# Attention with memory slots feeding a SiLU feed-forward: two weight tiles loaded into the unwritten half of w_in's tile, conversions moved into the prologue, Exp's table load ahead of k and v

## The chip, the cores and the metric

One core of one Trainium2 chip runs the whole kernel. The metric is the device time of one execution in microseconds (us), the median of a few runs. The kernel before takes 720.51 us (three runs, 720.13 to 721.42).

## The reference

```python
# q, k, v: [8, 8, 576, 64], phi: [8, 8, 576, 32], all float32
a = exp(phi - max(phi, axis=2)); a = a / (sum(a, axis=2) + 1e-9)   # softmax over the sequence
k_m = einsum('bhsm,bhsd->bhmd', a, k)                              # 32 memory slots per head
v_m = einsum('bhsm,bhsd->bhmd', a, v)
scores = matmul(q, k_m.T) / sqrt(64)
attn = softmax(scores, axis=-1)                                    # over the 32 slots
x = matmul(attn, v_m) -> [8 * 576, 512]                            # heads side by side
h = x @ w_in                                                       # [512, 2048]
out = (h * sigmoid(h)) @ w_out                                     # [2048, 512]
```

## The kernel before, in words

The kernel goes batch by batch (8 batches of 576 tokens), and within a batch over 16 slots `fc` of 128 feed-forward columns each. Instead of forming x, it multiplies w_in by v's memory first: `p_mm` (L540) makes the projection of a piece of w_in on PE into the PSUM tile `bg`, and `p_split` (L560) takes it to SBUF as a high part (ACT, L564) and a low part (DVE, L566), `pparts`. `ffn1` (L570) multiplies these with the high and low parts of the attention weights (`aparts`) into the PSUM tile `h`, of which there is one; `act` (L593) applies SiLU on ACT (`g`, `gleft`) and `split` (L586) makes `gparts` on DVE; `ffn2` (L605) multiplies these with `wo_hi` and `wo_lo` into `acc`. Each slot issues `ffn1` of its own columns, then `ffn2` of the slot before in two halves, and after each half the extra work that the table `events` holds for that slot (half slots are written .5).

The weights come as 64-bit words that hold float64 numbers. A weight tile ("i", j) or ("o", j) is 256 of w_in's columns or of w_out's rows, 1 MB in memory; there are eight of each kind. `w_load` (L120) loads a tile, or one half of it (`part`), into a buffer `raw`; there are three such buffers (`RAWB`), which the tiles use in turn. `w_conv` (L142) makes float32 of it in steps: step 0 is two ACT passes (L158, L159), step 1 two DVE passes (L162, L163). For w_out, a copy of the high part follows on ACT (L165) and, in step 2, a subtraction on DVE for the low part (L167). w_in's result goes into `win`, a constant tile for all 16 column groups, w_out's into `wo_hi` and `wo_lo`. `load_next` and `conv_next` (L172, L177) go through the tiles from j = 1 on in the order i1, o1, i2, o2, and so on; each `conv_next` loads a further tile behind its conversion. Loads with `few` set wait for the fifth load before them (`DEEP`).

Batch 0's attention, the prologue (L694 to L754), has a written order. `phi` is loaded through SP, k and v through ACT's queue, then q and the first weights through SP as `LOADS` (L43) lists them: i0 in two halves, both halves of q, o0 in two halves, and L, which is tile i1. Softmax over phi (`phi_max`, `phi_allmax`, `phi_sub`, `phi_exp`), the contraction with k and v (`e_mm`), the scores (`f_scores`, `f_copy`, `f_turn`), their softmax (`f_max`, `f_sub`, `f_exp`, `f_sum`, `f_norm`) and the way back (`f_back`, `f_high`, `f_low`) follow; `keep_warm` issues matmuls whose result isn't used. The instructions of PE and of SP keep the order of the text everywhere, those of DVE and ACT in the prologue; behind it, a planner orders DVE and ACT. Batch 1's attention is spread over the slots of batch 0, and so on for each batch. In batch 0 the tile of k and v is used in turn by `f_copy` too (tag `kv`).

Of the events of batch 0, these bear on the weights: the projection of w_in's tile j in slot max(1, 2j - 1.5); the second half of o0 in slot 0; the k-th `conv_next` (k from 0 to 13) in slot k.

Of the kernel before, what the change touches and what calls it, by code (L numbers as in the profile page):

```python
# [10 lines left out]
F32 = mybir.dt.float32  # L11
# [3 lines left out]
I64 = mybir.dt.int64  # L15
AF = mybir.ActivationFunctionType
# [3 lines left out]
P = 128  # L20
B, S, H, M, D = 8, 576, 8, 32, 64
HM = H * M
NR = H // 2
KVW = 2 * D + 1
DMODEL, DFF = 512, 2048
# [14 lines left out]
PHW = FULLC * HM + P  # L40
KVC = 2 * NR * KVW
RAWB = 3
LOADS = "i0 Q0 Q1 i1 o0 o1 L"  # L43
DEEP = 5


# [1 line left out]
def attn_ffn_kernel(  # L48
# [9 lines left out]
    nc = tc.nc  # L58
    const = ctx.enter_context(tc.tile_pool(name="const", bufs=1))
    sb = ctx.enter_context(tc.tile_pool(name="sb", bufs=2))  # L60
# [3 lines left out]
    ident = const.tile([P, P], F32, name="ident")  # L64
# [11 lines left out]
    def keep_warm(t, n):  # L76
        for _ in range(n):
            nc.tensor.matmul(
                t, dummy[:, :P], dummy.unsqueeze(1).broadcast_to([P, 2, 2 * P]),
                start=True, stop=True, skip_group_check=True,  # L80
            )
# [38 lines left out]
    def w_load(w, part=None, few=False):  # L120


        kind, j = w
        if w not in raws:
            shape = [P, 2, NR * P] if kind == "i" else [P, 2, DMODEL]
            raws[w] = sb.tile(shape, I64, tag="raw", name="raw", bufs=RAWB)
        if kind == "i":
            for k in range(2) if part is None else (part,):
                f = (2 * j + k) * P
                load(  # L130
                    raws[w][:, k].rearrange("p (r f) -> p r f", r=NR),
                    w_in[:, f : f + P].rearrange("(r p) f -> p r f", p=P),
                    few,
                )
        else:
            src = w_out[j * CW : (j + 1) * CW, :].rearrange("(r p) f -> p r f", p=P)
            load(w_part(raws[w], part), w_part(src, part), few)
# [4 lines left out]
    def w_conv(w, part=None, steps=(0, 1, 2)):  # L142
        kind, j = w
        words = raws[w].bitcast(U32).rearrange("p r (f t) -> p r f t", t=2)
        low, high = (w_part(words[:, :, :, t], part) for t in range(2))
        r = low.bitcast(I32)
        fc = slice(2 * j, 2 * j + 2) if part is None else slice(2 * j + part, 2 * j + part + 1)
        if kind == "i":
            to = win[:, fc].rearrange("p k r f -> p k (r f)")
            a = to.bitcast(I32)  # L150
        else:
            to = high.bitcast(F32)
            if 0 in steps:
                n, tag = (2, "cva") if part != 1 else (1, "cva1")
                cvas[w, part] = sb.tile([P, n, DMODEL], I32, tag=tag, name="cva", bufs=1)[:, : 2 if part is None else 1]
            a = cvas[w, part]
        if 0 in steps:
            nc.scalar.activation(a.bitcast(F32), high.bitcast(F32), AF.Prelu, scale=2.0**-112, alpha=-(2.0**32))  # L158
            nc.scalar.activation(r, low, AF.Copy, scale=2.0**-29)  # L159
        if 1 in steps:  # L160
            au = a.bitcast(U32)
            nc.vector.tensor_scalar(au, au, 3, None, op0=ALU.logical_shift_left)  # L162
            nc.vector.tensor_tensor(to.bitcast(I32), a, r, op=ALU.add)  # L163
            if kind == "o":
                nc.scalar.activation(wo_hi[:, fc], a.bitcast(F32), AF.Copy)  # L165
        if 2 in steps and kind == "o":
            nc.vector.tensor_tensor(wo_lo[:, fc], to, wo_hi[:, fc], op=ALU.subtract)  # L167

    to_load = iter([(k, j) for j in range(1, DFF // CW) for k in "io"])
# [2 lines left out]
    def load_next(few=False):  # L172
        w = next(to_load, None)
        if w is not None:
            w_load(w, None, few)
# [27 lines left out]
    def load_kv(b):  # L203
        queue = nc.scalar if b == 0 else None
        ts = []
        for c in range(FULLC):
            t = sb.tile([P, 2, NR, KVW], F32, tag="kv", name=f"kv{b}_{c}", bufs=FULLC)
            load(t.rearrange("p g r f -> p (g r f)"), kv[b, :, c * KVC : (c + 1) * KVC], queue=queue)
            ts.append(t)
        t = sb.tile([P, NR, KVW], F32, tag="kr", name=f"kr{b}", bufs=1)  # L210
        load(t.rearrange("p r f -> p (r f)"), kv[b, :, FULLC * KVC :], queue=queue)
        at[b]["kv"], at[b]["kr"] = ts, t

    def load_q(b, hf, few=False):
        t = sb.tile([P, NR, HALF], F32, tag="q", name=f"q{b}_{hf}", bufs=2)
        at[b]["q", hf] = t
        load(t.rearrange("p r s -> p (r s)"), qT[b, hf], few)
# [225 lines left out]
    def f_copy(u):  # L443
        if u == 0:
            first["left"] = sb.tile([P, P], F32, tag="mx", name="sleft", bufs=1)
        t = first["main", u] = sb.tile([P, 2, 2 * P], F32, tag="kv", name=f"sT{u}", bufs=FULLC)
        left = first["left"]
        nc.scalar.copy(t, first["st", u][:, :, : 2 * P])
        nc.scalar.copy(left.rearrange("p (g h f) -> p g h f", g=2, h=2)[:, :, u], first["st", u][:, :, 2 * P : HALF])

    def f_turn(u):
        main = first["main", u]
        if u == 0:
            t = ps.tile([P, 512], F32, tag="acc", name="firstu", bufs=NI)
        else:
            t = ps.tile([P, 2, 512], F32, tag="h", name="firstu", bufs=1).rearrange("p b f -> p (b f)")
        for c in range(2):
            for g in range(2):
                n = 2 * c + g
                nc.tensor.transpose(t[:, n * P : (n + 1) * P], main[:, g, c * P : (c + 1) * P], ident)  # L460
        if u:
            nc.tensor.transpose(t[:, 2 * HM : 2 * HM + P], first["left"], ident)
        first["ps", u] = t
# [23 lines left out]
    def f_sub(u):  # L487
        nc.vector.tensor_tensor(
            f_groups(f_sc(u)), f_groups(first["ps", u][:, : UW[u]]), f_bc(f_part(u, "mx", 2 * S // M), u),
            op=ALU.subtract,  # L490
        )

    def f_exp(u):
        nc.scalar.activation(f_sc(u), f_sc(u), AF.Exp, scale=SCALE)
# [36 lines left out]
    def f_low(u):  # L531
        nc.vector.tensor_tensor(f_to("alo", u), first["aT", u], f_to("ahi", u), op=ALU.subtract)
# [27 lines left out]
    def p_split(b, f, w, bg, steps=(0, 1)):  # L560
        hi, lo = pj[b, f // JW]
        c = slice(f % JW, f % JW + w)
        if 0 in steps:
            nc.scalar.activation(hi[:, :, c], bg[:, :, :w], AF.Copy)  # L564
        if 1 in steps:
            nc.vector.tensor_tensor(lo[:, :, c], bg[:, :, :w], hi[:, :, c], op=ALU.subtract)  # L566
# [71 lines left out]
    def ev(b, slot, fn, *a):  # L638
        events.setdefault((b, slot), []).append((fn, a))

    for b in range(B):
# [38 lines left out]
        if n + 1 < B:  # L680
            ev(b, sk, load_phi, n + 1)
        ev(b, 14, p_mm, n, 0, JW)
    ev(0, 0, w_conv, ("o", 0), 1)
    for k in range(DFF // CW * 2 - 2):
        ev(0, k, conv_next)

# [3 lines left out]
    whole = ExitStack()  # L692
    whole.enter_context(in_order(PE, SP))
    load_phi(0)  # L694
    load_kv(0)
    for c in LOADS.split():
        if c[0] == "Q":
            load_q(0, int(c[1]), True)
        elif c[0] == "L":
            load_next(True)  # L700
        else:
            w_load((c[0], 0), int(c[1]), True)
    w = [(("i", 0), 0), (("i", 0), 1), (("o", 0), 0)]
    idle = ps.tile([P, 2, 512], F32, tag="h", name="idle", bufs=1)[:, 0]
    with in_order(DVE, ACT) as last:
        keep_warm(idle, 9)
        for p in range(2):
            phi_max(0, (p,))
            phi_allmax(0, (p,))
            keep_warm(idle, (7, 8)[p])  # L710
        for p in range(2):
            phi_sub(0, (p,))
            phi_exp(0, (p,))
        e_mm(0)
        w_conv(*w[0], (0,))
        keep_warm(idle, 4)
        f_tr()
        w_conv(*w[0], (1,))
        keep_warm(idle, 2)
        f_scores(0)  # L720
        f_copy(0)
        f_turn(0)
        f_scores(1)
        f_copy(1)
        f_vt()
        f_turn(1)
        f_max(0)
        f_sub(0)
        f_exp(0)
        bg = p_mm(0, 0, P, False)  # L730
        spare = first["spare"] = ps.tile([P, 512], F32, tag="acc", name="spare", bufs=NI)
        keep_warm(spare, 10)
        f_max(1)
        f_sub(1)
        f_exp(1)
        nc.scalar.activation(tiny[:, :1], ident[:, :1], AF.Silu)
        f_sum(0)
        p_split(0, 0, P, bg, (0,))
        w_conv(*w[1], (0,))
        f_norm(0)  # L740
        f_back(0)
        f_sum(1)
        w_conv(*w[2], (0,))
        f_high(0)
        f_norm(1)
        f_back(1)
        p_split(0, 0, P, bg, (1,))
        f_low(0)
        f_high(1)
        f_high(2)  # L750
        f_low(1)
        f_low(2)
        w_conv(*w[1], (1,))
        w_conv(*w[2], (1, 2))  # L754
    load_phi(1)
    load_kv(1)
    load_q(1, 0)
# [87 lines left out]
```

## Time and profile before

| | |
|---|---|
| median of three runs | 720.51 us |
| the profiled execution | 721.51 us |
| its span, first to last instruction | 719.7 us |
| busy: PE, DVE, ACT | 97%, 51%, 36% of the span |
| mean granted clock of PE | 0.991 |
| moved by DMA | 60.14 MB, a mean of 84 GB/s |

PE is TensorE, PEld its weight loads, DVE VectorE, ACT ScalarE, SP the engine that issues most DMAs; ACTq and SPq are the queues of ACT and SP that issue a DMA. A row of a timeline begins with the start and the length in us and names engine, line, operation, written tile <- read tiles, and the shape; in brackets stands how long the engine had been idle before and what ended that. A row of waits gives the total, the count and the longest. A row of stages gives the stretch, its length, the busy time of PE, PEld, DVE, ACT and POOL with their instruction counts, the granted clock of PE as a share of full speed, the share of DMA time and GB/s.

### The profile page before, as it was taken

The numbers are of one execution on the slowest core, as the hardware profiler recorded it, in microseconds if no ns is written. First come the engines' busy times: TensorE is split into PE (matmuls) and PEld (weight loads), VectorE is DVE, ScalarE is ACT, GpSimd is POOL, SyncE is SP. The second block draws the span as 40 slices with busy tenths as digits, with TensorE's granted clock in tenths as the row PEclk, the third lists the DMA queues.
The fourth block names the chain that finished last, engine by engine and source line by source line (L and its number), as shares of the span: only waits on it lengthen the run. The fifth ranks groups of instructions, "written<-read, shape, count | busy, mean of one in ns | idle before, by whom it ended". The sixth has DMA issues, their size and how long they took to land.

```text
span 719.7 us, 11594 instructions
## 1 busy us (share of the span) xinstructions
PE 699.8 (97%) x4841; PEld 560.2 (78%) x4841; DVE 367.6 (51%) x659; ACT 258.7 (36%) x454; POOL 0.7 (0%) x6
## 2 busy tenths in 40 slices
PE   7679999999999999999999999999999999999997
PEld 3468678778887788887888878787888878888885
DVE  2788977537345373636436364545635456333322
ACT  2588944424124241524224242432422324232211
POOL 0000000000000000000000000000000000000000
PEclk9989999999999999999999999999999999999999
DMA  9867814232012320132110321132102000010002
GB/s 344 300 238 239 278 66 180 86 126 67 1 59 70 112 66 1 58 134 67 34 59 15 134 66 34 59 133 67 34 1 73 2 1 1 0 60 1 1 1 73
DMA packets 25444, 60.14 MB, mean 84 GB/s; under 512 B 2096, under 2 KB 10416, under 8 KB 25392
## 3 DMA queue, kind: packets, MB, share of 16 engines
q1 hardware_dynamic: 24672, 57.02, 22.6%
q10 hardware_dynamic: 720, 2.38, 0.9%
q8 instruction: 38, 0.62, 0.4%
q14 instruction: 14, 0.11, 0.0%
HBM read 49.95 MB, written 9.44 MB: 83 GB/s over the span
## 4 chain that ended last, share of the span: by engine, by line
PE 85%; DVE 4%; ACT 3%; DMA 1%; issue 0%; SPq 0%; ACTq 0%
PE acc L610 45%; PE h L580 26%; PE accleft L610 6%; PE bg L550 4%; PE bg L300 2%; PE bg L344 1%; DMA raw<-in_w_in 1%; ACT phi L288 1%; DVE gparts L590 1%; ACT L596 1%; DVE phi L280 1%; ACT pparts L564 0%; ACT g L596 0%; PE bg L308 0%; ACT win L158 0%
## 5 line engine op out<-in xcount | busy, mean ns | idle before, releaser
L610 PE MATMUL acc<-wo_hi,gparts 128*128 128x512 f32 x1024 | 354.0, 398 | 0.0
L610 PEld LDWEIGHTS acc<-wo_hi,gparts 128*128 128x128 f32 x1024 | 192.9, 188 | 67.0 <-issue 31.8
L580 PEld LDWEIGHTS h<-aparts,pparts 128*128 128x128 f32 x1536 | 218.2, 190 | 16.9 <-ACT gleft L598 3.3
L580 PE MATMUL h<-aparts,pparts 128*128 128x288 f32 x1536 | 228.2, 298 | 1.8 <-ACT aparts L529 1.1
L610 PE MATMUL acc<-wo_lo,gparts 128*128 128x512 f32 x512 | 201.8, 394 | 0.0
L596 ACT ACTIVATE g<-h 128x512 f32<-128x512 f32 x128 | 76.4, 597 | 306.5 <-issue 177.6
L589 DVE CAST gparts<-g 128x512 fp32r<-128x512 f32 x128 | 54.5, 426 | 221.0 <-ACT g L596 220.1
L610 PEld LDWEIGHTS acc<-wo_lo,gparts 128*128 128x128 f32 x512 | 96.4, 188 | 14.4
L590 DVE TENSOR_TENSOR gparts<-g,gparts 128x512 fp32r<-128x512 f32 x128 | 88.2, 689 | 10.4
L566 DVE TENSOR_TENSOR pparts<-bg,pparts 128x1024 fp32r<-128x1024 f32 (+2 forms) x37 | 39.7, 1074 | 39.8 <-ACT pparts L564 39.8
L564 ACT ACTIVATE pparts<-bg 128x1024 fp32r<-128x1024 f32 (+2 forms) x37 | 33.5, 906 | 32.4 <-PE bg L550 32.4
L610 PE MATMUL accleft<-wo_hi,gparts 128*128 128x512 f32 x128 | 40.6, 389 | 0.0
L550 PE MATMUL bg<-win,kvT 64*32 64x512 f32 (+2 forms) x592 | 36.2, 546 | 3.9 <-DVE win L163 3.9
L598 ACT ACTIVATE gleft<-h 128x64 f32<-128x64 f32 x128 | 27.9, 218 | 0.0
L610 PEld LDWEIGHTS accleft<-wo_hi,gparts 128*128 128x128 f32 x128 | 24.0, 188 | 4.9
L616 ACT ACTIVATE o<-acc 128x512 f32<-128x512 f32 x32 | 19.1, 598 | 18.8 <-PE acc L610 10.7
L610 PE MATMUL accleft<-wo_lo,gparts 128*128 128x512 f32 x64 | 24.9, 389 | 0.0
L596 ACT ACT_TABLE_LOAD x14 | 18.0, 1283 | 8.1 <-PE h L580 7.9
L550 PEld LDWEIGHTS bg<-win,kvT 64*32 64x32 f32 x592 | 6.8, 105 | 17.2 <-issue 17.0
L159 ACT ACTIVATE raw<-raw 128x1024 int32<-128x1024 uint32 (+1 forms) x18 | 19.1, 1061 | 0.0
L589 DVE CAST gparts<-gleft 128x512 fp32r<-128x512 f32 x16 | 6.8, 426 | 20.7 <-PE accleft L610 12.2
L382 DVE TENSOR_REDUCE ssm<-sc 128x36 f32<-128x1152 f32 x7 | 9.5, 1354 | 9.6 <-ACT sc L378 9.6
(115 smaller groups left out, 362.7 us busy)
## 6 DMA issues: line engine op xcount, KB each, us to landing
kv<-in_kv SPq DMA_DIRECT2D x28, 516.0 KB, 5.9
q<-in_q SPq DMA_DIRECT2D x16, 576.0 KB, 3.8
raw<-in_w_in SPq DMA_DIRECT2D x16, 512.0 KB, 5.0
out<-o SPq DMA_DIRECT2D x32, 256.0 KB, 2.0
raw<-in_w_out SPq DMA_DIRECT2D x7, 1024.0 KB, 5.7
phi<-in_phi SPq DMA_DIRECT2D x7, 576.0 KB, 3.7
kv<-in_kv ACTq DMA_DIRECT2D x4, 516.0 KB, 6.4
kr<-in_kv SPq DMA_DIRECT2D x7, 258.0 KB, 6.6
```

What stands on the lines that cost most here:

```text
L159: nc.scalar.activation(r, low, AF.Copy, scale=2.0**-29)
L300: nc.tensor.matmul(pt[p][M * r : M * (r + 1), :KVW], e[:, p, c, M * r : M * (r + 1)], kvt[c][:, p, r], start=c == 0, stop=False, skip_grou ...
L550: nc.tensor.matmul(bg[M * r : M * (r + 1), p, :w].rearrange("p (k f) -> p k f", f=P), kvT[D * p : D * (p + 1), 1, r], win[D * p : D * (p + ...
L564: nc.scalar.activation(hi[:, :, c], bg[:, :, :w], AF.Copy)
L566: nc.vector.tensor_tensor(lo[:, :, c], bg[:, :, :w], hi[:, :, c], op=ALU.subtract)
L580: nc.tensor.matmul(h[:, hf, :HALF], wt[:, p, fs], a[:, p, sl], start=n == 0, stop=n == 5)
L589: nc.vector.tensor_copy(ghi, g32)
L590: nc.vector.tensor_tensor(glo, g32, ghi, op=ALU.subtract)
L596: nc.scalar.activation(g32.rearrange("p (h f) -> p h f", h=2), h[:, :, :w], AF.Silu)
L598: nc.scalar.activation(gleft[:, fc, o : o + LEFT].rearrange("p (h f) -> p h f", h=2), h[:, :, w:HALF], AF.Silu)
L610: nc.tensor.matmul(acc[key], gt[:, cs], wt[:, fc], start=fc == 0 and n == 0, stop=fc == NFC - 1 and n == 2)
L616: nc.scalar.activation(o, acc.pop(key), AF.Copy)
```

## The change

Two of the early weight tiles, o1 and i2, get a home of their own: instead of a `raw` buffer, their words are loaded into the column groups 8 to 11 and 12 to 15 of `win`, which are written only when w_in's tiles 4 to 7 are converted. `LOADS` issues them right behind i1, ahead of batch 1's phi, k, v and q. The two `load_next` behind the prologue then load o2 and i3.

The `conv_next` events move one slot ahead: the first two stand in slot 0, the k-th from there on in slot k - 1.

In the prologue, both steps of i0's second half go ahead: step 0 behind the first `f_copy`, step 1 behind the first `f_sub`. Step 0 of o0's first half goes behind the first `f_exp`, its step 1 ahead of the first `f_low`, its step 2 stays at the end. Step 0 of o0's second half, so far in slot 0, comes into the prologue behind `p_split`, and slot 0 keeps its steps 1 and 2. The copy to `wo_hi` belongs to step 2 now.

Exp's table is loaded by a one-column activation ahead of the loads of k and v, which stand in the written order of ACT from then on. The counts of `keep_warm` ahead of and between the maxima of phi are 11, 5 and 6 instead of 9, 7 and 8.

```diff
-LOADS = "i0 Q0 Q1 i1 o0 o1 L"
+LOADS = "i0 Q0 Q1 i1 o0 o1 L L L"
+HOMES = {("o", 1): 8, ("i", 2): 12}
...
         if w not in raws:
-            shape = [P, 2, NR * P] if kind == "i" else [P, 2, DMODEL]
-            raws[w] = sb.tile(shape, I64, tag="raw", name="raw", bufs=RAWB)
+            if w in HOMES:
+                home = win[:, HOMES[w] : HOMES[w] + 4].rearrange("p k r f -> p (k r f)")
+                raws[w] = home.bitcast(I64).rearrange("p (k f) -> p k f", k=2)
+            else:
+                raws[w] = sb.tile([P, 2, DMODEL], I64, tag="raw", name="raw", bufs=RAWB)
...
-            if kind == "o":
-                nc.scalar.activation(wo_hi[:, fc], a.bitcast(F32), AF.Copy)
         if 2 in steps and kind == "o":
+            nc.scalar.activation(wo_hi[:, fc], a.bitcast(F32), AF.Copy)
             nc.vector.tensor_tensor(wo_lo[:, fc], to, wo_hi[:, fc], op=ALU.subtract)
...
-    ev(0, 0, w_conv, ("o", 0), 1)
+    ev(0, 0, w_conv, ("o", 0), 1, (1, 2))
     for k in range(DFF // CW * 2 - 2):
-        ev(0, k, conv_next)
+        ev(0, max(0, k - 1), conv_next)
...
-    load_kv(0)
-    for c in LOADS.split():
...
     with in_order(DVE, ACT) as last:
-        keep_warm(idle, 9)
+        nc.scalar.activation(tiny[:, :1], ident[:, :1], AF.Exp)
+        load_kv(0)
+        for c in LOADS.split():
...
+        keep_warm(idle, 11)
...
-            keep_warm(idle, (7, 8)[p])
+            keep_warm(idle, (5, 6)[p])
...
         f_copy(0)
+        w_conv(*w[1], (0,))
         f_turn(0)
...
         f_sub(0)
+        w_conv(*w[1], (1,))
         f_exp(0)
+        w_conv(*w[2], (0,))
         bg = p_mm(0, 0, P, False)
...
         p_split(0, 0, P, bg, (0,))
-        w_conv(*w[1], (0,))
+        w_conv(("o", 0), 1, (0,))
         f_norm(0)
         f_back(0)
         f_sum(1)
-        w_conv(*w[2], (0,))
         f_high(0)
...
         p_split(0, 0, P, bg, (1,))
+        w_conv(*w[2], (1,))
         f_low(0)
...
-        w_conv(*w[1], (1,))
-        w_conv(*w[2], (1, 2))
+        w_conv(*w[2], (2,))
```

More of the change, by code (lines that the diff above doesn't have):

```diff
@@ L694, in attn_ffn_kernel @@
     load_phi(0)
-    load_kv(0)
-    for c in LOADS.split():
[L697 to L702, printed above, removed]
     w = [(("i", 0), 0), (("i", 0), 1), (("o", 0), 0)]
@@ L705, in attn_ffn_kernel @@
     with in_order(DVE, ACT) as last:
-        keep_warm(idle, 9)
+        nc.scalar.activation(tiny[:, :1], ident[:, :1], AF.Exp)
+        load_kv(0)
+        for c in LOADS.split():
+            if c[0] == "Q":
+                load_q(0, int(c[1]), True)
+            elif c[0] == "L":
+                load_next(True)
+            else:
+                w_load((c[0], 0), int(c[1]), True)
+        keep_warm(idle, 11)
         for p in range(2):
```

## The prediction

> **What bounds the kernel now.** I read the page's totals, then the table of stages, the waits of TensorE (PE) by releaser, and the timelines of single engines. Totals and stages (columns: stretch, length, busy PE, PEld, DVE, ACT, POOL, granted clock, DMA share, GB/s):
> ```profile
> span 719.7 us, 11594 instructions
> PE 699.8 (97%) x4841; PEld 560.2 (78%) x4841; DVE 367.6 (51%) x659; ACT 258.7 (36%) x454; POOL 0.7 (0%) x6
> ...
> 30.00:35.00 5.00, 4.14 (x30) 3.16 (x31) 4.26 (x9) 1.89 (x6) 0.00 (x0) 0.66 0.22 71
> ...
> 40.00:45.00 5.00, 4.64 (x30) 3.74 (x31) 4.95 (x8) 3.81 (x5) 0.00 (x0) 0.66 0.99 328
> 50.00:55.00 5.00, 4.46 (x31) 3.89 (x32) 4.37 (x6) 3.57 (x6) 0.00 (x0) 0.66 0.62 219
> 75.00:80.00 5.00, 3.40 (x21) 2.80 (x21) 4.75 (x7) 5.00 (x8) 0.00 (x0) 1.00 0.91 287
> ...
> 31.00:82.00 51.00, 45.18 (x356) 36.24 (x356) 44.32 (x71) 42.17 (x57) 0.00 (x0) 0.90 0.70 240
> 82.00:122.00 40.00, 40.00 (x289) 31.27 (x289) 31.71 (x44) 21.51 (x32) 0.00 (x0) 1.00 0.44 157
> ```
> Over the whole span PE is the bound, and from 82 us on it is solid: there only PE's own work counts, and the change takes none away. Before 82 us PE idles and also loses clock: a clock of 0.66 over 5 us is 5 x 0.34 / 0.5 = 3.4 us at half speed, which costs 1.7 us of full-speed work. The second and third such stretch come right behind a PE gap:
> ```profile
> PE bg L550 <- DVE win L163: 3.9, 2, 2.0
> ...
> 40.36 0.67 PE L550 MATMUL bg<-win,kvT 64*32 64x256 f32 x16 [1.84 <-DVE win L163]
> 50.54 0.67 PE L550 MATMUL bg<-win,kvT 64*32 64x256 f32 x16 [2.03 <-DVE win L163]
> 79.63 0.44 PE L330 MATMUL bg<-ident,kvn 128*128 128x128 f32 x2 [1.60 <-DVE pparts L566]
> ```
> So three gaps: two projections wait for the conversion of w_in's tiles 1 and 2, the third for a DVE subtraction. The 1.6 us gap costs no clock (1.00 in its stage). The conversions and the load behind those gaps:
> ```profile
> 35.12 0.66 ACT L158 ACTIVATE cva<-raw 128x512 f32<-128x512 f32 x1
> 36.25 1.16 ACT L158 ACTIVATE win<-raw 128x1024 f32<-128x1024 f32 x1
> 37.81 1.15 ACT L159 ACTIVATE raw<-raw 128x1024 int32<-128x1024 uint32 x1
> 38.99 1.23 DVE L163 CUSTOM_DVE_ANT_0 win<-raw,win 128x2048 uint16<-128x2048 uint16 x1 [0.26 <-ACT raw L159]
> ...
> 38.76 0.93 SPq L86 DMA_DIRECT2D raw<-in_w_in  x2
> 44.30 1.17 ACT L158 ACTIVATE win<-raw 128x1024 f32<-128x1024 f32 x1 [1.19 <-DMA raw<-in_w_in]
> ```
> Tile 1 is late because ACT first does w_out's second half (35.12 to 36.25). Tile 2 is late because its load is issued only at 38.76, when a raw buffer comes free, and lands at 44.3.
>
> **The start, part by part.**
> ```profile
> 0.73 2.19 ACTq L86 DMA_DIRECT2D kv<-in_kv  x4
> 5.50 1.28 ACT L291 ACT_TABLE_LOAD   x1 [5.50 <-DMA phi<-in_phi]
> 26.64 0.20 ACT L736 ACTIVATE tiny<-ident 128x1 f32<-128x1 f32 x1
> phi<-in_phi SPq DMA_DIRECT2D x7, 576.0 KB, 3.7
> 8.29 0.43 DVE L229 TENSOR_TENSOR mt<-phi 128x256 f32<-128x256 f32 x1 [0.88 <-DMA phi<-in_phi]
> 1.35 4.02 PE L78 MATMUL idle<-ident 128*128 128x512 bf16 x9 [1.35 <-POOL ident masks.py:199]
> 6.60 0.48 PE L241 MATMUL firstm<-ident,mx 128*128 128x128 f32 x1 [1.22 <-DVE mx L232]
> 8.05 2.96 PE L78 MATMUL idle<-ident 128*128 128x512 bf16 x7
> 10.85 0.27 PE L241 MATMUL firstm<-ident,mx 128*128 128x128 f32 x1
> 11.83 1.89 PE L78 MATMUL idle<-ident 128*128 128x512 bf16 x8
> 13.65 2.32 PE L300 MATMUL first<-kv,phi 128*32 128x129 f32 x64
> 11.06 1.45 SPq L86 DMA_DIRECT2D raw<-in_w_out  x2
> ```
> Exp's table load moves ahead of the five k/v issues on ACT. It was free at 5.50 (Exp itself comes just ahead of the contraction at 13.65); now it and a one-column Exp hold the k/v issues back by 1.28 + 0.20 = 1.5 us. The w_out issue at 11.06 waits for the last k/v piece, so that piece lands near 11.0, and 12.5 after; the contraction needs it at its end, later than that, so the delay is hidden. The gated issues on SP wait for the fifth load ahead of them, so the 1.5 us passes down to q and the weights: the second issue of the pair at 13.62 (fence further down) waits for q's second half, here near 15.1, in after near 16.6, and its scores are copied at 21.32 only. With k/v out of the way, phi should land in about the 3.7 us that a whole phi takes later: near 4.4 instead of 8.29 for its last part. Then PE's own warm-up matmuls rule: 11 instead of 9 ahead of the first transpose, 5 instead of 7 ahead of the second. At half speed one is 2.96 / 7 = 0.42 us, so 11 from 1.35 end near 6.0, and the first transpose comes 0.6 ahead of its 6.60. Two warm-ups fewer (0.84) would put the second 1.4 earlier; the seven at 8.05 ended only at 11.0, 0.15 behind the 10.85 of the transpose after them, so I take **1.2 us**: the second at 9.65, the contraction at 12.45 instead of 13.65. Bounds: 1.2 gained, or 0.1 lost if the clock isn't up by then (the last 6 warm-ups at 0.42 instead of 1.89 / 8 = 0.24, +1.1, and part of the 2.32 us contraction at half speed, +0.2 or more).
>
> The ScalarE: Activation LUTs page of the Trainium skill (section "What ACT_TABLE_LOAD costs") counts a drain of about 1.4 us beside each table load; by that the k/v pieces would land about 2.9 us later, 13.9, still ahead of the contraction's end. The trace has no such drain: the 1.28 us load is the whole of it.
>
> Then the conversions in gaps:
> ```profile
> 21.32 0.58 ACT L448 COPY sT<-firsts 128x512 f32<-128x512 f32 x1 [1.35 <-PE firsts L435]
> 24.59 0.74 ACT L494 ACTIVATE fsc<-fsc 128x640 f32<-128x640 f32 x1 [1.88 <-DVE fsc L488]
> 22.87 0.82 DVE L483 TENSOR_REDUCE fmx<-firstu 128x20 f32<-128x640 f32 x1 [0.85 <-PE firstu L462]
> 29.24 1.04 ACT L529 ACTIVATE aparts<-firsta 128x512 fp32r<-128x512 f32 x2
> 29.84 1.29 DVE L532 TENSOR_TENSOR aparts<-firsta,aparts 128x512 fp32r<-128x512 f32 x2 [1.03 <-ACT aparts L529]
> 31.25 0.42 DVE L162 TENSOR_SCALAR win<-win 128x512 uint32<-128x512 uint32 x1
> 31.39 2.77 PE L580 MATMUL h<-aparts,pparts 128*128 128x288 f32 x10 [0.35 <-DVE aparts L532]
> ```
> A half tile costs ACT 36.25 - 35.12 = 1.1 for its pair, and DVE 0.42 + 0.6 (half of a whole tile's 1.23), some 1.1 with the step between them. ACT's pair after the first score copies goes into its 1.35 gap, the second pair into 1.88: both at nothing; if a gap closes, up to 1.1 each on the softmax chain. DVE's pair goes into 0.85, so the second row maximum is 0.3 late. One ACT pair instead of two now stands ahead of the high parts at 29.24, which come 1.1 earlier on that count and 1.2 for the start, but DVE's other pair (1.1) now stands ahead of the low parts and fills its 1.03 gap. So the low parts, which release the first feed-forward matmuls at 31.39, gain 1.2 - 0.3 - 0.2 (what the pair overruns its gap) = **0.7 us** (bounds: 0.6 lost with the slow clock, 1.2 gained). SP's queue: phi, k, v and q of batch 1 now stand behind 2 MB of weights, at 398 GB/s some 5 us (next fence). Batch 1's phi is used first at 44.68, so this is covered. The two weight loads behind batch 1's wait for raw buffers that the prologue's conversions free; behind them on SP stand only further weights.
> ```profile
> 20.00:25.00 5.00, 4.14 (x50) 2.11 (x51) 3.48 (x5) 1.81 (x5) 0.00 (x0) 1.00 1.06 398
> 44.68 0.68 DVE L229 TENSOR_TENSOR mt<-phi 128x512 f32<-128x512 f32 x1
> 13.62 1.82 SPq L86 DMA_DIRECT2D raw<-in_w_in  x2
> ```
>
> **The main loop, part by part.** The two home tiles put w_out's tile 1 and w_in's tile 2 right behind w_in's tile 1, whose issue is at 13.62; with 1 MB each at 398 GB/s they land by some 26 to 27 us, 17 us ahead of 44.3. Tile 2's load is no longer late; what is late next is ACT and DVE. For tile 1: w_out's second half is off ACT's queue (1.1), and the first h comes 0.7 earlier, so ACT's second pass ends at 37.81 + 1.15 - 1.1 - 0.7 = 37.2 and DVE's 1.23 at 38.4, against PE asking at 40.36 - 1.84 = 38.5, or 37.8 after the earlier start: gap 1 shrinks from 1.84 to 0.6, and to 0 if ACT starts the tile in its idle time ahead of the first SiLU. Tile 2 follows a slot earlier than before and should be ready before PE asks near 44: gap 2 (2.03) goes. The homes are overwritten by w_in's tiles 4 to 7, whose conversions stand several tiles behind theirs in the same queues: no wait. The w_out high copy on ACT moves with the last step, at its old cost. Each half-speed stretch behind them (1.7) goes with its gap. Together at most 1.84 + 2.03 + 2 x 1.7 = 7.3.
>
> Against that, the engines that convert. From 31 to 82 DVE is busy 44.32 of 51 and ACT 42.17. The prologue takes 2 x 1.1 from DVE, leaving 42.1, and 1.1 from ACT. If the stretch shrinks by 7.3 to 43.7, DVE must be busy 96% of it, as much as in its fullest row (4.95 of 5), and queues in order don't keep that up next to PE's own demands. Bounds: at 95% (the 4.75 of the stage at 75) it needs 42.1 / 0.95 = 44.3, a gain of 6.7; at today's 44.32 / 51 = 87% 48.4, a gain of 2.6. Conversions may slip behind 82, where DVE has 8 us free of 40, so I take the upper half: 93%, 45.3, **a gain of 5.7**. I keep the third gap at 1.6 within this: the same queue makes it.
>
> On the clock, the page TensorE: Matmul & The Clock Gate of the Trainium skill ("What's actually happening") has half speed only after a whole idle window of about 3.4 us. By that the gaps of 1.84 and 2.03 cost no clock, and mending them would bring 3.9 and not 7.3. By the rows here, both gaps are followed by 0.66 at once; what remains of that reading is rival (e).
>
> **Sum.** 0.7 + 5.7 = 6.4 us. The profiled execution took 721.51 (719.7 is its span, 1.8 lies around it), 1.0 above the median 720.51: 715.1 against it, **714.1** against the median.
>
> **Rivals.**
> (a) *More*: the start gains 1.2, both gaps and their half-speed stretches go (7.3), and the third gap too (1.6): 10.1, 710.4. For it: all three have one cause, late conversions. Against: DVE would need over 96%.
> (b) *The bound moves to DVE*: its queue stays at 87%, main loop 2.6 and start 0.7: 717.2. For it: 4.95 of 5 already from 40 to 45. Against: conversions have slack at the far end.
> (c) *The change doesn't do what it says*: tiles land early, but ACT's queue still converts them behind the same SiLUs, so the gaps stay; only 0.7 of the start: 719.8, no difference that can be told. For it: tile 1, landed early already, was late all the same. Against: w_out's half tile is off ACT.
> (d) *Slower*: two conversions now stand in slot 0 and each later one a slot earlier. In DVE's queue a conversion that waits for ACT holds the split parts behind it, as at 79.63. With such a 1.6 us gap in each of slots 1 to 6, 6 x 1.6 = 9.6 stands against 0.7 + 7.3: +1.6, 722.1. It decides from the sixth gap on (five are 8.0, even). For it: DVE and ACT over 80% busy; against: only one such gap before.
> (e) *The half speed stays*: it follows something else than the two gaps (the small projections' matmuls, say), and only the gaps go: 0.7 + 3.9 = 4.6, 715.9. Against: both later rows of 0.66 hold or follow such a gap, and the 1.00 stages between have none over 1.6. This is where the clock gate's page would come out.
>
> **How the numbers follow.** Forecast 0.52 (its own range 711.5 to 716.5), (a) 0.11, (b) 0.15, (c) 0.08, (d) 0.10, (e) 0.04. Faster by over 0.2% (1.4 us, about what a measurement of this kernel can tell): forecast, (a), (b) and (e), 0.82; same (c), 0.08; slower (d), 0.10. The range 710.0 to 719.3 holds the forecast, (a), (b) and (e) and so about 8 in 10.
>
> **What would show it.** In the profile of after: no phi wait at 8.29 and the contraction near 12.5; first feed-forward matmuls running through near 30.7; PE's wait for DVE's conversion under 0.5 us in place of 3.9; no clock of 0.66 between 37 and 55 (one near 31 may stay, or shift); DVE over 90% between 31 and 75; PE solid from about 76. I am wrong if the contraction isn't earlier, if new PE waits for DVE or ACT over 2 us stand between 35 and 75, or if the clock falls without a gap.

## The result, and the profile after

The changed kernel takes 716.01 us, the kernel before beside it 720.33: a ratio of 0.9946, 95% interval 0.9921 to 0.9970. Timed a second time, on another chip, it was 717.12 against 719.93, 0.9957 (0.9944 to 0.9970). So the change brings 3 to 4 us. The profiled execution took 718.63 us (span 716.8), 2.6 above the median: executions of one kernel differ by as much, and the clock, below, is one reason. The pair of profiles is 2.9 us apart, so it shows less than the medians do.

Totals and stages of the changed kernel (columns as before the change):

```profile
span 716.8 us, 11588 instructions
...
25.00:30.00 5.00, 2.45 (x10) 1.90 (x11) 4.90 (x12) 4.40 (x8) 0.00 (x0) 0.78 1.06 390
30.00:35.00 5.00, 5.00 (x34) 3.69 (x34) 4.74 (x9) 4.61 (x8) 0.00 (x0) 0.54 1.03 408
40.00:45.00 5.00, 4.06 (x28) 3.31 (x33) 4.57 (x10) 2.62 (x4) 0.00 (x0) 1.00 0.78 288
50.00:55.00 5.00, 4.97 (x30) 4.12 (x29) 4.31 (x8) 3.27 (x4) 0.00 (x0) 1.00 0.96 306
75.00:80.00 5.00, 5.00 (x21) 4.47 (x22) 3.95 (x6) 2.48 (x5) 0.00 (x0) 0.66 0.76 252
...
31.00:82.00 51.00, 46.45 (x365) 36.22 (x365) 42.38 (x66) 39.61 (x56) 0.00 (x0) 0.93 0.75 263
```

The two stretches of half speed behind the old gaps are gone (1.00 at 40 and at 50), but the one near 30 is twice as long, and there is a new one at 75. PE's waits, and its rows where they fall (lines have moved by 3):

```profile
PE bg L333 <- DVE pparts L569: 2.1, 1, 2.1
PE bg L303 <- DVE pparts L569: 1.3, 1, 1.3
PE h L583 <- DVE pparts L569: 1.0, 1, 1.0
...
11.03 0.43 PE L303 MATMUL first<-kv,phi 128*32 128x129 f32 x8
29.13 2.77 PE L583 MATMUL h<-aparts,pparts 128*128 128x288 f32 x10 [0.37 <-DVE aparts L535]
40.94 1.34 PE L583 MATMUL h<-aparts,pparts 128*128 128x288 f32 x8 [1.00 <-DVE pparts L569]
60.90 1.97 PE L303 MATMUL bg<-kv,phi 128*32 128x129 f32 x64 [1.30 <-DVE pparts L569]
75.00 0.44 PE L333 MATMUL bg<-ident,kvn 128*128 128x128 f32 x2 [2.06 <-DVE pparts L569]
```

The wait for the converted w_in (3.9 us in two gaps) is gone altogether. In its place PE waits three times for the low part of a projection, and twice more for 0.2 us. The starts of the feed-forward's first matmuls, read from PE's two timelines, show where the lead was won and given back:

| slot | before | after | lead |
|---|---|---|---|
| 1 | 35.28 | 33.34 | 1.9 |
| 2 | 43.35 | 39.26 | 4.1 |
| 3 | 51.14 | 45.53 | 5.6 |
| 5 | 62.84 | 56.36 | 6.5 |
| 6 | 69.79 | 64.67 | 5.1 |
| 8 | 81.30 | 77.57 | 3.7 |
| 9 | 86.31 | 83.22 | 3.1 |
| 11 | 96.68 | 93.86 | 2.8 |

The lead grows to 6.5 us as the two gaps go, and 3.7 of it is lost again by slot 11. About 2.0 of this are waits (the 1.3, the 0.25 at 86.71, and 2.06 where the kernel before had 1.60); the other 1.7 is the half-speed stretch behind the last of the three waits. The chain of the changed kernel that ended last (start, length, what) says what made the waits:

```profile
47.04 1.24 DVE wo_lo L170
48.30 0.37 SPq L87
...
48.72 4.88 DMA raw<-in_w_in
...
53.68 1.15 ACT win L162
...
55.45 1.28 ACT L291
56.75 1.17 ACT phi L291
...
62.51 1.24 DVE win L167
...
63.76 7.04 DMA raw<-in_w_out
...
70.91 1.14 ACT cva L162
...
73.11 1.23 DVE raw L167
74.34 0.61 DVE pparts L569
...
75.00 0.44 PE bg L333 x2
```

It is a ring: a conversion ends and frees one of the three raw buffers, SP issues the load that waited for it, the load lands 4.9 or 7.0 us later, ACT stands waiting for it, and what is queued behind, the high and the low part of a projection, comes late to PE. Loads aren't all of it: from 55.45 to 58.77 Exp's table load (1.28), batch 1's Exp (1.17) and a copy to `wo_hi` also stand ahead of a high part on ACT. Behind w_in's tile 2 the kernel is back on three buffers; as this chain reads, the two homes moved the head of the line, not its pace.

### The profile page after: what moved, and what is told of

Read it like the earlier page. It is cut to its first block, busy times and chain, and to the rows that moved or that the text cites. A ratio compares the mean times of both kernels' runs of the same rounds, so it can differ in the third digit from the quotient of the medians.

```text
span 716.8 us, 11588 instructions
## 1 busy us (share of the span) xinstructions
PE 698.6 (97%) x4839; PEld 559.1 (78%) x4839; DVE 366.9 (51%) x659; ACT 258.8 (36%) x455; POOL 0.7 (0%) x6
## 4 chain that ended last, share of the span: by engine, by line
PE 83%; DVE 4%; ACT 4%; DMA 2%; issue 0%; SPq 0%; ACTq 0%; DVEq 0%
PE acc L613 45%; PE h L583 25%; PE accleft L613 6%; PE bg L553 4%; PE bg L303 2%; PE bg L347 1%; DMA raw<-in_w_out 1%; ACT L599 1%; DMA raw<-in_w_in 1%; ACT phi L291 1%; DVE gparts L593 1%; DVE raw L167 1%; DVE phi L283 1%; ACT pparts L567 0%; ACT raw L163 0%
## 5 line engine op out<-in xcount | busy, mean ns | idle before, releaser
L163 ACT ACTIVATE raw<-raw 128x1024 int32<-128x1024 uint32 (+1 forms) x16 | 16.8, 1049 | 0.0
L303 PE MATMUL bg<-kv,phi 128*32 128x129 f32 x448 | 13.8, 275 | 1.3 <-DVE pparts L569 1.3
```

The costliest lines, as they stand in the source:

```text
L303: nc.tensor.matmul(pt[p][M * r : M * (r + 1), :KVW], e[:, p, c, M * r : M * (r + 1)], kvt[c][:, p, r], start=c == 0, stop=False, skip_grou ...
```

## The experiments

All ratios are against the kernel before, timed on the same chip beside the run; 0.001 is 0.7 us.

**The start alone.** The kernel before with Exp's table ahead of the k and v issues, and the warm-up counts 11, 5, 6.

```diff
-    load_kv(0)
-    for c in LOADS.split():
...
+        nc.scalar.activation(tiny[:, :1], ident[:, :1], AF.Exp)
+        load_kv(0)
+        for c in LOADS.split():
...
-        keep_warm(idle, 9)
+        keep_warm(idle, 11)
...
-            keep_warm(idle, (7, 8)[p])
+            keep_warm(idle, (5, 6)[p])
```

> The kernel before with only the start changed: Exp's table and the one-column Exp ahead of the k and v issues, warm-up counts 11, 5 and 6. Theory (the start is a rigid shift: everything behind it, loads of weights included, follows the prologue): the contraction begins near 11.0 to 12.4 instead of 13.65, both gaps before the projections stay near 1.8 and 2.0 us, and the time falls by the whole shift, 1.2 to 2.3 us, to 718.0 to 719.1. Rival (the prologue's gain is eaten by the gaps, which wait for loads at fixed times): the gaps grow by the shift and the time stays at 720.

Measured: 719.36 against 719.79, ratio 0.9986 (0.9976 to 0.9996): 1.0 us (0.3 to 1.7). The waits for the converted w_in and the start of the contraction:

```profile
PE bg L550 <- DVE win L163: 3.7, 2, 2.1
...
12.52 0.43 PE L300 MATMUL first<-kv,phi 128*32 128x129 f32 x8
```

Both gaps stay and the start passes through, as a rigid shift would. Its size lies below the 1.2 to 2.3 us of the theory, though the interval reaches into them.

**The order alone**, with the old warm-up counts, in the kernel before.

```diff
-    load_kv(0)
-    for c in LOADS.split():
...
+        nc.scalar.activation(tiny[:, :1], ident[:, :1], AF.Exp)
+        load_kv(0)
+        for c in LOADS.split():
...
```

> The kernel before with Exp's table and the one-column Exp ahead of the k and v issues, and the warm-up counts 9, 7 and 8 as before. Theory (the earlier start of the contraction needs both parts: phi lands earlier, but seven and eight warm-ups then hold PE): the k and v issues begin near 1.3, phi's first part lands near 3.6, and the contraction still begins near 12 to 13, so the time is 719.3 to 720.3, no difference that can be told. Rival (the order alone does it): the contraction begins near 11 to 12 and the time is that of the start's changes together, 0.9986 of the kernel before, or less.

Measured: 718.87 against 720.16, 0.9981 (0.9972 to 0.9990): 1.4 us (0.7 to 2.0). In its profile, of its slowest execution (720.14), the contraction began at 13.05, with the eight warm-ups ahead of it mostly at half speed (2.84 us, where the kernel before took 1.89). But the time fell by as much as with the counts changed too: the counts have no effect that these runs can tell, and the theory that both parts are needed falls.

**The change without its start.**

```diff
+    load_kv(0)
+    for c in LOADS.split():
...
-        nc.scalar.activation(tiny[:, :1], ident[:, :1], AF.Exp)
-        load_kv(0)
-        for c in LOADS.split():
...
-        keep_warm(idle, 11)
+        keep_warm(idle, 9)
...
-            keep_warm(idle, (5, 6)[p])
+            keep_warm(idle, (7, 8)[p])
```

> The changed kernel with the start as before: k and v first, Exp's table where it was, warm-up counts 9, 7 and 8. Theory (the start is worth about 2.3 us by the changed kernel's trace): 718.3. Rival (the prediction's size of the start, 0.7 us, with the rest a matter of how the clock's windows fall): 716.7.

Measured: 717.95 against 719.79, 0.9974 (0.9964 to 0.9984). Against the 0.9946 and 0.9957 of the whole, the start is worth some 1.2 to 2 us, between theory and rival.

**The homes alone**, in the kernel before.

```diff
-LOADS = "i0 Q0 Q1 i1 o0 o1 L"
+LOADS = "i0 Q0 Q1 i1 o0 o1 L L L"
+HOMES = {("o", 1): 8, ("i", 2): 12}
...
```

> The kernel before with only the two home tiles and the longer list of loads. Theory (gap 2 is a late load, gap 1 is a busy ACT): the gap of 2.03 us and its half-speed stretch go (3.7 us), the gap of 1.84 us stays, time 716.6. Rival (conversions are ordered the same way, so an earlier load changes nothing): both gaps stay, 720.

Measured: 718.28 against 719.79, 0.9974 (0.9963 to 0.9985). One of the two waits is left, and there is a new one of 1.3 us for SiLU's output:

```profile
PE bg L554 <- DVE win L167: 1.6, 1, 1.6
```

So gap 2 was a late load, and gap 1 wasn't. The gain of 1.9 us (1.1 to 2.7) is about the size of the gap; the half-speed stretch that the theory added to it didn't come.

**The change without the homes.**

```diff
-LOADS = "i0 Q0 Q1 i1 o0 o1 L L L"
-HOMES = {("o", 1): 8, ("i", 2): 12}
+LOADS = "i0 Q0 Q1 i1 o0 o1 L"
...
```

> The changed kernel without home tiles: w_in's tile 1 is the last early load, the rest goes through three raw buffers. Theory (w_in's tile 2 waits for the raw buffer of w_out's tile 0, converted near 34, so it lands near 40 and is converted near 43 to 45): the wait for the converted tile 2 is back with 0.5 to 2 us, 716.8 to 718.0. Rival (with the earlier conversions its raw buffer comes free early enough, and the homes are worth nothing): 716.

Measured: 718.88 against 719.93, 0.9991 (0.9975 to 1.0007): without the homes no gain that can be told is left. The wait for tile 2's conversion isn't back, so the theory's place was wrong, and with the earlier conversions gap 2 stays closed without the homes. PE waits for low parts five times instead (0.4 to 1.8 us each). In the profiled execution, 721.95 and so 3.1 us above the median of this kernel, the prologue paid too. ACT's pair that now stands ahead of the second score copies waited for its load:

```profile
19.59 0.66 ACT L158 ACTIVATE win<-raw 128x512 f32<-128x512 f32 x1 [1.53 <-DMA raw<-in_w_in]
```

In the changed kernel that same load was there in time (its pair ran at 17.46 with no wait), so moving a conversion into a gap cost nothing there, but it hangs on a landing.

**The prologue's conversions back where they stood.**

```diff
-    ev(0, 0, w_conv, ("o", 0), 1, (1, 2))
+    ev(0, 0, w_conv, ("o", 0), 1)
...
         f_copy(0)
-        w_conv(*w[1], (0,))
...
         f_sub(0)
-        w_conv(*w[1], (1,))
         f_exp(0)
-        w_conv(*w[2], (0,))
...
-        w_conv(("o", 0), 1, (0,))
+        w_conv(*w[1], (0,))
...
+        w_conv(*w[2], (0,))
...
-        w_conv(*w[2], (1,))
...
-        w_conv(*w[2], (2,))
+        w_conv(*w[1], (1,))
+        w_conv(*w[2], (1, 2))
```

> The changed kernel with the conversions of w_in's and w_out's first tiles where they stood before (behind f_sum, f_norm and at the prologue's end; the second half of w_out's tile 0 whole in slot 0). Theory (ACT and DVE behind the prologue are what makes w_in's tile 1 late): the wait of the projection for the converted tile 1 is back with 1 to 1.8 us, and the first feed-forward matmuls start no later; 717.0 to 718.0. Rival (the home tiles do it all): 716.

Measured: 717.78 against 719.93, 0.9967 (0.9956 to 0.9979).

```profile
PE bg L553 <- DVE win L167: 1.7, 1, 1.7
```

The wait for tile 1 is back with 1.7 us. Gap 1 was ACT and DVE behind the prologue, and the moved conversions close it.

**The slots back.**

```diff
-        ev(0, max(0, k - 1), conv_next)
+        ev(0, k, conv_next)
```

> The changed kernel with the conversions' slots as before (conversion k in slot k). Theory (loads and prologue do the work, the slots only give the order in which the planner sees the conversions): within 0.7 us of the changed kernel, 715.3 to 716.7. Rival 1 (the earlier slots make the new PE waits of 1.0, 1.3 and 2.1 us for the projections' low parts): these waits shrink and it is 713 to 714.5. Rival 2 (the earlier slots are what closes the gaps): the waits for the converted w_in come back, 718 or more.

Measured: 716.5 against 719.79, 0.9951 (0.9937 to 0.9964): the slots do nothing that can be told. PE's waits change places and not their sum (these two and two shorter ones, 4.3 us of idling against 4.8):

```profile
PE h L583 <- ACT gleft L601: 1.8, 1, 1.8
PE bg L333 <- DVE pparts L569: 1.7, 1, 1.7
```

**The changed kernel and the kernel before, profiled again**, for the clock.

> The changed kernel once more, beside the kernel before on the same chip. Theory (the clock's half-speed windows fall where the phase of the window meets an idle PE, so their number varies from execution to execution, and they didn't go with the two gaps): the profile shows the same three PE waits (about 1.0, 1.3 and 2.1 us) but other half-speed windows; time 715.5 to 716.5. Rival (half speed is fixed by the gaps): again two windows near 28 and one behind the 2.1 us gap near 76.

> The kernel before once more, for a second profile. Theory (half speed follows only where a gap lies mostly within one window of the clock's gate, whose phase is free): the gaps of 1.8 and 2.0 us are there again, but not both are followed by half speed. Rival (as the prediction had it): both are.

The changed kernel took 717.12 against 719.93 here, above the 715.5 to 716.5 of the theory. In its profile PE waits 1.0, 1.3, 0.5 and 1.8 us for low parts, the last at a place where the first profile has 0.25; half speed holds from 27.95 to 34.77 and nowhere behind it. So the windows differ, as the theory had it, but so do the waits. The kernel before: gaps of 1.83 and 2.06 us, both followed by half speed, as the rival had it. The two gaps lie 10.2 us apart, three windows of 3.41 us, so that if one falls within a window, the other does too.

The windows below begin and end where the changes of the granted clock lie, at whole multiples of 3.41 us from them. They are, in turn: two of the kernel before; the first of the two at half speed and the one of the last wait in the changed kernel; one of its second profile; one of the kernel without the homes; and two neighbours of the start alone.

```profile
37.95:41.36 3.41, 1.57 (x21) 0.72 (x20) 3.11 (x6) 3.41 (x5) 0.00 (x0) 1.00 0.40 114
48.19:51.60 3.41, 1.38 (x21) 0.68 (x20) 3.15 (x5) 2.01 (x3) 0.00 (x0) 1.00 0.49 137
```
```profile
27.78:31.20 3.42, 2.92 (x10) 2.58 (x11) 3.42 (x8) 3.42 (x5) 0.00 (x0) 0.50 1.03 411
72.16:75.57 3.41, 1.35 (x8) 0.83 (x7) 3.07 (x4) 3.41 (x5) 0.00 (x0) 1.00 1.03 411
```
```profile
82.56:85.97 3.41, 1.61 (x21) 0.75 (x19) 1.72 (x4) 3.02 (x5) 0.00 (x0) 1.00 0.23 88
```
```profile
86.41:89.82 3.41, 1.62 (x21) 0.83 (x20) 2.51 (x4) 3.41 (x6) 0.00 (x0) 1.00 0.00 0
```
```profile
44.70:48.11 3.41, 2.19 (x10) 1.47 (x8) 3.01 (x7) 2.07 (x4) 0.00 (x0) 1.00 0.97 323
48.11:51.52 3.41, 2.50 (x29) 2.10 (x30) 3.04 (x4) 3.02 (x4) 0.00 (x0) 1.00 0.52 170
```

Where PE was busy for 1.57, 1.38 and 1.35 of 3.41 us (0.46, 0.40, 0.40), the next window ran at half speed. At 1.61 it didn't and at 1.62 it did (both 0.47). The gap of 2.13 us in the start alone, longer than either gap of the kernel before, cost no clock: the edge at 48.11 cut it in two, and both windows were busy for 0.64 and more. The old third gap of 1.60 us was cut in the same way, at 78.91.

Over all profiles here, each of the 22 full-speed windows with PE busy for 0.46 or less was followed by half speed, and none with 0.56 or more. Behind 32 us none with 0.48 or more was either; in the prologue the border is less sharp, with four windows of 0.53 to 0.55 that were followed by half speed and others of 0.50 to 0.54 that weren't.

**A third home**: w_in's tile 4 loaded where tile 2 had been. In this kernel the load of tile 4 overwrote tile 2's words before they were converted, so a part of w_in is wrong in it.

```diff
-HOMES = {("o", 1): 8, ("i", 2): 12}
+HOMES = {("o", 1): 8, ("i", 2): 12, ("i", 4): 12}
```

> The changed kernel with a third home: w_in's tile 4 is loaded where tile 2 was, so every later load comes one conversion earlier. Theory (the 2.1 us wait at the batch's transposes comes from a conversion at the head of ACT's and DVE's queues whose load is late): this wait shrinks below 0.7 and the time is 713.5 to 714.5. Rival (the planner takes an earlier load as leave to put more conversions ahead of the projections' low parts on DVE; in its order four tiles now stand ahead of one): PE waits over 2 us for a low part near 45 to 55, and it is 717 or more.

Measured: 727.09 against 719.93, 1.0094 (1.0081 to 1.0107). The load of tile 4 into tile 2's home, and behind it the conversion of tile 2:

```profile
36.20 2.98 SPq L87 DMA_DIRECT2D win<-in_w_in  x2
51.24 1.13 ACT L162 ACTIVATE win<-win 128x1024 f32<-128x1024 f32 x1
```

The planner put tile 2's conversion behind three later tiles, and PE waited 10.6 us for it. That shows how much of the time hangs on the planner's order, but nothing on whether faster loads would end the ring. A home that no earlier tile uses wasn't tried.

**The written order**: DVE and ACT keep the order of the text through batch 0. In the second version w_out's tile 1 is converted in slot 1 as well.

```diff
+    written = ExitStack()
+    written.enter_context(in_order(DVE, ACT))
     for b in range(B):
         if b == 1:
+            written.close()
             whole.close()
```
```diff
-        ev(0, max(0, k - 1), conv_next)
+        ev(0, max(min(1, k), k - 1), conv_next)
```

> The changed kernel with DVE's and ACT's instructions kept in the order of the text through all of batch 0, where a planner orders them otherwise. In the text each projection's low part stands right behind the conversion of its own half slot, so no later conversion stands ahead of it. Theory (the PE waits of 1.0, 1.3 and up to 2.1 us for low parts are made by conversions that the planner put ahead of them): these waits sum to under 1.5 us between 45 and 90, and the time is 713.5 to 715.5 where the changed kernel takes 716 to 717. Rival (DVE and ACT are simply full, whatever the order): the waits change places, SiLU comes later behind two conversions in slot 0, and it is 716.5 to 719.

> As the run with the written order, and w_out's tile 1 converted in slot 1 and not in slot 0, so that the second SiLU doesn't wait behind it. Theory (queue order): 0.5 to 1.5 us less than with the written order alone, from the wait ahead of the third slot's matmuls. Rival (full engines): the same within 0.5.

Measured: 724.79 against 720.10, 1.0053 (1.0037 to 1.0069), and 726.36, 1.0078 (1.0053 to 1.0103). Stage and waits of the first:

```profile
31.00:76.00 45.00, 38.37 (x319) 29.25 (x317) 33.55 (x53) 31.17 (x43) 0.00 (x0) 0.91 0.53 188
...
PE bg L303 <- DVE pparts L569: 2.2, 1, 2.2
PE h L583 <- ACT gleft L601: 1.9, 1, 1.9
PE h L583 <- DVE pparts L569: 1.7, 1, 1.7
PE bg L244 <- DVE pparts L569: 1.2, 1, 1.2
PE bg L553 <- DVE win L167: 1.1, 1, 1.1
```

Both theories fall, and so does the first rival: the time lies above its range. The two versions can't be told apart, their intervals overlap. The low parts stand right behind the conversions of their own half slot, and PE waits for them longer (some 5 us in three waits, where the changed kernel has 4.4). A wait for the converted w_in is back too, 1.1 us here and 3.2 in two with the second version. And the engines are not full, DVE is busy 33.55 of 45 us. The reading that fits is that a queue in the text's order stands still while ACT and DVE wait for each other, so that conversions end later and the loads behind them start later (188 GB/s, against 263 in the changed kernel over the same stretch); no run takes these apart. The planner's order was worth more than it cost.

## Why the prediction was right, and where it wasn't

The sign and the range held: 716.0 and 717.1 against 714.1 forecast, with 710.0 to 719.3. The change in time, 3 to 4 us, is about half of the 6.4 us predicted, or a little more. By its steps:

- *The two gaps and their causes* were right. Gap 2 went with the homes, gap 1 with the prologue's conversions, each shown by the run that does or undoes that part alone (the moved conversions closed gap 2 as well, where there were no homes). Together 3.9 us of PE's waiting is gone.
- *The half speed behind the gaps, 2 x 1.7 us, was the largest term that failed.* The two stretches went, but others came. The first profiles of the two kernels hold three windows at half speed each: before one near 31 and two behind the gaps, after two near 29 and one behind the new wait at 75. The second profiles hold three and two. The window at 27.78 was busy for 2.92 of 3.42 us and yet the clock stayed down through the next one. On the page TensorE: Matmul & The Clock Gate, section "What's actually happening", the Trainium skill says that the window runs freely and doesn't start with the kernel. The profiles agree: from the kernel's first instruction, half speed first begins at 31.12 us in one profile of the kernel before and at 29.16 in the other, which is no multiple of 3.41 apart. I had set a gap and the half speed behind it together as cause and effect, from two cases that were one, three windows apart. Rival (e) describes the first pair of profiles better than the forecast does: no half speed was saved on balance.
- *A whole idle window*, which the same page of the Trainium skill asks for ahead of half speed, isn't needed here: 1.84 and 1.83 us of idling within one window were enough in the two profiles of the kernel before.
- *The start*: 0.7 us forecast, timed alone 1.0 (0.3 to 1.7), and 1.2 to 2 by the run that takes it out: the forecast lies at the low end, too near to be called wrong. The first pair of profiles has 31.39 - 29.13 = 2.26 for it, the second pair 29.70 - 29.40 = 0.30. The two profiles of the kernel before alone lie 1.7 us apart at this place, so much of the 2.26 can be chance. The step that didn't hold is the price of the warm-ups: I took 0.42 us each from a profile in which full speed first came at 10.6 us. In the second profile of the same kernel seven took 1.67 us, 0.24 each, and in the changed kernel, with full speed from 7.3 on, five took 1.24. The k and v issues came only 0.6 us later, not 1.5, and phi's last part wasn't near 4.4: it landed at 8.75 with the start alone, and by 6.69 and at 7.53 in the two profiles of the changed kernel. Below, the changed kernel first, then two rows of the kernel before and one of the changed kernel, each from its second profile.

```profile
0.73 1.28 ACT L701 ACT_TABLE_LOAD   x1 [0.73 <-PEq L799]
1.34 0.86 ACTq L87 DMA_DIRECT2D kv<-in_kv  x2
2.03 0.20 ACT L701 ACTIVATE tiny<-ident 128x1 f32<-128x1 f32 x1
...
6.69 0.41 DVE L232 TENSOR_TENSOR mt<-phi 128x256 f32<-128x256 f32 x1
7.37 1.24 PE L79 MATMUL idle<-ident 128*128 128x512 bf16 x5
```
```profile
6.98 1.67 PE L78 MATMUL idle<-ident 128*128 128x512 bf16 x7
29.70 2.77 PE L580 MATMUL h<-aparts,pparts 128*128 128x288 f32 x10 [0.27 <-DVE aparts L532]
```
```profile
29.40 2.77 PE L583 MATMUL h<-aparts,pparts 128*128 128x288 f32 x10 [0.37 <-DVE aparts L535]
```

- *The engines that convert* were the right place to look for the loss, with the wrong price and cause. I took 1.6 us off for full queues and kept the third gap at 1.6. In the profile the three waits for low parts make 4.4 us where the old three gaps made 5.5, and DVE was busy 42.38 of 51 us, 83% (88% in the second profile), where it was 87% before and the forecast needed 93%. So DVE didn't fill up; the waits show it standing for ACT, and the chain ACT for loads that wait for raw buffers. That this ring sets the pace from 45 to 86 us rests on the chain and on the waits; no run took it away. Two of the prediction's signs failed here: DVE was at 85% between 31 and 75 and not over 90%, and a new wait of over 2 us, named there as a sign of being wrong, ends at 75.00.
- *The pairs of profiles add up*, each in its own way. The first: 2.26 for the start, 5.5 - 4.8 = 0.7 for the waits in the loop (4.8 with two of 0.2), nothing for the clock: 3.0 against the 2.9 measured. The second: 0.3 for the start and 5.6 - 4.8 = 0.8 for the waits; of the 2.5 us between the spans 1.4 are left, beside one half-speed window fewer.
- *Rival (d)*, a low part queued behind a conversion, is what happened, three times and not six. *Rival (a)* is out, *(c)* too: the homes alone gave 1.9 us. *Rivals (e)*, 715.9, and *(b)*, 717.2, come nearer to the two measured times than the forecast; but (b) has a full DVE for its reason, which the traces don't show.

## What to carry to other kernels

Loading the first pieces early closes the first gaps, but behind them, as the chain here reads, the pace is set by how soon buffers come free: ask at which tile the extra room ends, and price the gap that returns there. A throttled stretch behind a gap belongs to the gap and to where the clock's window lies; count it by its chance, not in full. A second profile of the same kernel tells how much of a difference is chance: here the first one overstated the start. A part that a change moves is measured by undoing it alone: here two edits, the slots and the warm-up counts, did nothing that could be told.

## What the runs showed of the hardware

A DMA issued from ACT's queue doesn't wait for the engine's work ahead of it: the first two k and v issues began at 1.34 us, while the table load ran from 0.73 to 2.01 and the activation before them in the text began at 2.03. By the times, they waited for no more than that activation's own wait, the identity matrix that PE's first warm-up waits for too, at 1.36.

The clock goes down after a window of 3.41 us in which PE was busy for 0.46 of the time or less (22 of 22 in the profiles here), and behind the prologue it stays up after 0.48 and more; PE need not idle for a whole window. It comes up again after a half-speed window that is busy for 0.90 or more, and stays down after one of 0.75 to 0.85 (eight cases). So the same gap costs up to 1.7 us more, half of 3.41, or nothing, by where the window's edge falls.

One landing varies enough to matter: w_out's load took 7.04 us in one profile of the changed kernel and 5.49 in the other, and the wait at the transposes behind it was 2.06 and 0.5 us.
